# Second matmul of experts 1 to 7 by seven products of block sums, with output sums shared among DVE, ACT and POOL

## Chip, cores, metric

One core of one Trainium2 chip. The metric is the device time of one execution in microseconds (us); lower is better. Engines are named as in the profile: PE (matmul), PEld (weight load), DVE (vector), ACT (scalar), POOL (GpSimd), SP. SBUF and PSUM are the two memories in which the kernel declares its tiles; its matmuls of the expert stage write to PSUM tiles of 128 by 512 float32 ("banks").

## The reference, cut to what matters

A sparse attention (about the first 150 us, not touched in substance) makes `x` of 3072 tokens by 512. Then comes a dense mixture of 8 experts, with a routing matrix `P` that is normalised in eight rounds:

```python
def _moe_ref(x, w_gate, w1, w2):
    N, D, E, F = 3072, 512, 8, 1024
    ...                                  # P: [N, E]
    for e in range(E):
        h = np.maximum(x @ w1[e], 0.0)   # [N, F]
        ye = h @ w2[e]                   # [N, D]
        out += P[:, e:e + 1] * ye
    return out
```

## The kernel before

Every operation is a unit with a cost for each engine that may run it. A list scheduler (`Plan.order`) then fixes the order of instructions on each engine, and semaphores are added for the data.

For experts 1 to 7, `x @ w1` is already formed from seven products (the Strassen-Winograd scheme) over pairs of 512-token blocks `t1, t2` and halves of F. One "quad" is 128 columns of each half of F: seven products of two 512-column matmuls each, in place of eight. DVE sums two blocks for some products; PE adds most products in PSUM; a product that is needed twice is copied out ("snap") and added by DVE together with the relu:

```python
        def add_relu(e, p, q, blk):          # DVE: relu(PSUM + snapshot in SBUF)
            nc.vector._custom_dve(dve_ops.TENSOR_ADD_SAT, out=hidden(e, p, q, blk),
                                  in0=at[src, e, p, q][:], in1=at.pop(("snap", n, e, p, q))[:],
                                  s0=3.0e38, s1=0.0)
```

`h @ w2` is an ordinary product: for each 128 tokens, eight matmuls of 512 columns into one PSUM bank, and one DVE pass that adds `P * y` to the float32 sum `out_acc` in SBUF:

```python
        def project(e, p, c, fs, d=slice(0, DM)):
            ...
            for f in fs:
                nc.tensor.matmul(yp[:, d], lhsT=hb[e, p, q // 2][:, q % 2, blk, o:o + 128],
                                 rhs=w2s[e][:, f, d], start=(f == 0), stop=(f == KF - 1))

        def accumulate(e, p, c, d=slice(0, DM)):
            nc.vector.scalar_tensor_tensor(out=out_acc[:, t, d], in0=at.pop(("y", e, p, c, d.start))[:, d],
                                           scalar=P_sb[:, t, e:e + 1], in1=out_acc[:, t, d],
                                           op0=ALU.mult, op1=ALU.add)
```

There are 7 experts with 3 pairs of token blocks each: 21 (expert, pair). The very last 128 tokens are done in two halves of 256 columns.

The softmax here doesn't subtract the row's maximum and nothing guards it: scores larger than these inputs give would overflow.

## Time and profile before

700.39 us (median of 3; 699.55 to 701.0).

| | before |
|---|---|
| span of the profiled run | 699.8 us |
| first product of expert 1 starts | 151.9 us |
| PE work in the expert stage, about 544 us by the pitch below | 1176 matmuls of 512 columns for x @ w1, 1344 for h @ w2 (8 of them made as 16 of 256) |
| start to start, 512 columns, own weight load each | 215.8 ns |
| time PE lost beyond that pitch in the expert stage | 0.2 us |

The last two rows come from the start times of single matmuls in the trace: the interval from each start to the next, less the pitch of a matmul of that width as these starts show it (215.9 ns for 512 columns, where the 2512 intervals of the kernel before have a mean of 215.8 and a median of 216, and 109.3 for 256, where they take 109 or 110). This matters because the profile's "busy" of PE is made of modelled ends that overlap: a 512-column matmul is recorded as 379 ns long though the next starts 216 ns later, so short gaps are covered. I call this sum of lost intervals "PE gaps" below.

From the profile page of the kernel before: busy time of each engine with its share of the span, and the engines' shares of the chain of waits.

```profile
span 699.8 us, 10429 instructions
...
PE 690.7 (99%) x4128; PEld 338.4 (48%) x4130; DVE 435.5 (62%) x851; ACT 290.3 (41%) x505; POOL 91.4 (13%) x132
...
PE 91%; DMA 4%; POOL 2%; DVE 1%; issue 0%; SPq 0%; DVEq 0%; POOLq 0%
```

PE is 91% of the chain. The windows view of the same kernel (busy us of each engine with the number of instructions, granted clock, DMA) for a steady stretch of 78 us, which is one expert, and for the whole expert stage:

```profile
core 0: us, PE busy (x) PEld busy (x) DVE busy (x) ACT busy (x) POOL busy (x), PEclk, DMA share, GB/s
344.00:422.00 78.00, 78.00 (x363) 35.41 (x362) 43.31 (x65) 27.99 (x49) 1.64 (x2) 1.00 0.17 28
150.00:700.00 550.00, 546.00 (x2538) 248.07 (x2536) 311.45 (x474) 193.48 (x334) 9.81 (x12) 1.00 0.17 35
```

PE is busy all the time, DVE 43.3 of 78 us. The groups of instructions in the expert stage that the argument uses (count, busy us, mean ns of one, then idle time before):

```profile
L752 PE MATMUL yps<-w,h 128*128 128x512 f16 x1336 | 349.7, 379 | 0.0
...
L757 DVE SCALAR_TENSOR_TENSOR out_acc<-yps,P_sb,out_acc 128x512 f32<-128x512 f32 x167 | 124.7, 747 | 140.2 <-PE yps L752 140.1
L738 DVE CUSTOM_DVE_ANT_0 h<-pA,snap 128x512 f16<-128x512 f32 x84 | 57.8, 688 | 4.3 <-PE pA L721 0.3
...
L703 DVE TENSOR_TENSOR wsum<-w 128x1024 f16<-128x1024 f16 x12 | 8.2, 681 | 0.0
...
L752 PE MATMUL yps<-w,h 128*128 128x256 f16 x16 | 1.9, 273 | 0.0
```

The DVE operation (`wsum`, 1024 f16 elements) takes 0.68 us. And one line of the timeline of PE at the end of the run, with start and length:

```profile
694.20 0.93 PE L752 MATMUL yps<-w,h 128*128 128x256 f16 x7
```

Seven half-width matmuls with seven weight loads, one recorded as 273 ns, take 0.93 us: (0.93 - 0.273)/6 = 0.109 us from start to start. Half the columns, half the time.

The waits of PE in the expert stage come to this one line (who waited for what: us in total, times, longest):

```profile
...
PEld L721 <- issue: 0.2, 1, 0.2
```

### The profile page before, as it was taken

The page shows a single profiled execution, that of the slowest core. Times are in us where ns is not written, and L with a number is a line of the kernel's source. Part 1 is how long each engine was busy: PE and PEld are TensorE (multiplying, and loading weights), DVE is VectorE, ACT ScalarE, POOL GpSimd, SP SyncE. Part 2 cuts the span into 40 slices and gives each one's busy share as a digit, 9 for nine tenths or more (in the row PEclk, how much of TensorE's full clock was granted, in tenths as well). Part 3 has the DMA queues.
Part 4 walks back from the last instruction along what each step waited for, and adds up shares of the span by engine and source line. Part 5 has one row for each costly group of instructions (what it writes and reads, how often), then busy time and mean ns, then how long its engine had stood idle before and what let it go on. Part 6 is the DMA issues. An engine that isn't in the chain of part 4 may idle for free.

```text
span 699.8 us, 10429 instructions
## 1 busy us (share of the span) xinstructions
PE 690.7 (99%) x4128; PEld 338.4 (48%) x4130; DVE 435.5 (62%) x851; ACT 290.3 (41%) x505; POOL 91.4 (13%) x132
## 2 busy tenths in 40 slices
PE   8999999999999999999999999999999999999997
PEld 4666656554444444444444444444444444444443
DVE  7779877989765555475455654564555655455453
ACT  6667775554333333333333333333333333333330
POOL 7899622000000000000000000000000000000000
PEclk9999999999999999999999999999999999999999
DMA  9999933525003040204003030304003120001223
GB/s 170 160 144 145 134 64 59 93 28 93 1 1 60 1 60 1 47 14 61 1 0 61 3 58 1 60 1 61 0 1 61 19 42 1 0 1 45 91 80 146
DMA packets 95392, 36.24 MB, mean 52 GB/s; under 512 B 76016, under 2 KB 88816, under 8 KB 95344
## 3 DMA queue, kind: packets, MB, share of 16 engines
q0 software_dynamic: 77520, 25.99, 34.6%
q1 hardware_dynamic: 17152, 9.45, 5.6%
q8 instruction: 32, 0.52, 0.3%
q10 hardware_dynamic: 672, 0.15, 0.1%
q14 instruction: 16, 0.13, 0.1%
HBM read 52.45 MB, written 6.29 MB: 84 GB/s over the span
## 4 chain that ended last, share of the span: by engine, by line
PE 91%; DMA 4%; POOL 2%; DVE 1%; issue 0%; SPq 0%; DVEq 0%; POOLq 0%
PE yps L752 41%; PE pA L721 21%; PE pQ L721 10%; PE pR L721 5%; PE yps L228 5%; PE hps L223 4%; DMA w<-in_moe_w_dram 1%; DMA kT<-kst 1%; DMA Ve<-vx 1%; DMA vx<-in_v_dram 1%; PE sg L345 1%; PE av L437 1%; PE av L431 1%; PE ss L450 0%; POOL vx L287 0%; PE tkq L301 0%
## 5 line engine op out<-in xcount | busy, mean ns | idle before, releaser
L752 PE MATMUL yps<-w,h 128*128 128x512 f16 (+1 forms) x1352 | 351.5, 378 | 0.0
L757 DVE SCALAR_TENSOR_TENSOR out_acc<-yps,P_sb,out_acc 128x512 f32<-128x512 f32 (+1 forms) x169 | 125.6, 744 | 141.0 <-PE yps L752 140.9
L752 PEld LDWEIGHTS <-h 128*128 128x128 f16 x1352 | 132.3, 98 | 158.0
L219 ACT COPY snap<-pA 128x512 f32<-128x512 f32 x166 | 97.1, 585 | 143.2 <-PE pA L721 143.1
L214 ACT ACTIVATE h<-pA 128x512 f16<-128x512 f32 x83 | 49.6, 597 | 171.0 <-PE pA L721 171.0
L738 DVE CUSTOM_DVE_ANT_0 h<-pQ,snap 128x512 f16<-128x512 f32 x84 | 57.8, 688 | 77.8 <-PE pQ L721 77.2
L721 PEld LDWEIGHTS <-wsum 128*128 128x128 f16 x672 | 65.8, 98 | 79.3
L721 PE MATMUL pA<-xsum,wsum 128*128 128x512 f16 x336 | 99.6, 379 | 0.0
L721 PEld LDWEIGHTS <-w 128*128 128x128 f16 x504 | 49.3, 98 | 59.5 <-issue 0.2
L738 DVE CUSTOM_DVE_ANT_0 h<-pR,snap 128x512 f16<-128x512 f32 x84 | 57.5, 685 | 11.2 <-ACT snap L219 11.2
L738 DVE CUSTOM_DVE_ANT_0 h<-pA,snap 128x512 f16<-128x512 f32 x84 | 57.8, 688 | 4.3 <-PE pA L721 0.3
L219 ACT COPY snap<-pQ 128x512 f32<-128x512 f32 x83 | 48.5, 584 | 21.0 <-PE pQ L721 20.7
L721 PE MATMUL pQ<-xsum,wsum 128*128 128x512 f16 x168 | 50.0, 379 | 0.0
L721 PE MATMUL pA<-xsum,w 128*128 128x512 f16 x168 | 50.0, 379 | 0.0
L721 PE MATMUL pA<-xT,w 128*128 128x512 f16 x168 | 50.0, 379 | 0.0
L721 PE MATMUL pQ<-xT,wsum 128*128 128x512 f16 x168 | 50.0, 379 | 0.0
L721 PE MATMUL pR<-xT,w 128*128 128x512 f16 x168 | 50.0, 379 | 0.0
L223 PE MATMUL hps<-xT,w 128*128 128x384 f16 x256 | 48.0, 326 | 1.1 <-DMA w<-in_moe_w_dram 1.0
L228 PE MATMUL yps<-w,h 128*128 128x512 f16 x192 | 46.3, 379 | 0.0
L204 POOL DMA_DIRECT2D w<-in_moe_w_dram x11 | 8.4, 770 | 244.9 <-PE pA L721 241.9
L210 POOL DMA_DIRECT2D w<-in_moe_w_dram x8 | 7.1, 890 | 185.2 <-PE yps L752 121.3
L214 ACT ACTIVATE h<-hps 128x384 f16<-128x384 f32 x55 | 27.0, 491 | 10.2 <-PE hps L223 9.4
(127 smaller groups left out, 503.5 us busy)
## 6 DMA issues: line engine op xcount, KB each, us to landing
w<-in_moe_w_dram POOLq DMA_DIRECT2D x15, 1024.0 KB, 8.7
out_dram<-out_acc SPq DMA_DIRECT2D x23, 256.0 KB, 2.0
qst<-in_q_dram POOLq DMA_DIRECT2D x32, 96.0 KB, 5.4
vx<-in_v_dram POOLq DMA_DIRECT2D x15, 192.0 KB, 6.2
kst<-in_k_dram POOLq DMA_DIRECT2D x24, 96.0 KB, 5.7
w<-in_moe_w_dram POOLq DMA_DIRECT2D x4, 256.0 KB, 8.7
kst<-in_k_dram POOLq DMA_DIRECT2D x3, 192.0 KB, 4.6
Ve<-vx SPq DMA_DIRECT2D x32, 10.2 KB, 5.5
```

Of the source, the lines that this page charges most:

```text
L204: nc.gpsimd.dma_start(out=w1s[e][:, :, part * fw:(part + 1) * fw], in_=moe_w1[e].rearrange("(dk p) f -> p dk f", p=128)[:, :, part * fw:(p ...
L210: nc.gpsimd.dma_start(out=w2s[e][:], in_=moe_w2[e].rearrange("(fk p) d -> p fk d", p=128))
L214: nc.scalar.activation(out=out, in_=in_, func=AF.Relu, bias=0.0, scale=1.0)
L219: (nc.scalar.copy if eng == "ACT" else nc.vector.tensor_copy)(out=out, in_=in_)
L223: nc.tensor.matmul(hp[:, 0:n], lhsT=w1s[e][:, dk, f * 128:(f + 1) * 128], rhs=xT[:, dk, t0:t0 + n], start=(dk == 0), stop=(dk == KD - 1))
L228: nc.tensor.matmul(yp[:, d], lhsT=h[:, f, c * 128:(c + 1) * 128], rhs=w2s[e][:, f, d], start=(f == 0), stop=(f == KF - 1))
L345: nc.tensor.matmul(dst, lhsT=kT[r][p0:p0 + 64, g * 128:(g + 1) * 128], rhs=qT[r][p0:p0 + 64, g * 128 + l0:g * 128 + l1], start=True, stop= ...
L431: nc.tensor.matmul(av[:, o + j * VD:o + (j + 1) * VD], lhsT=em[:, j, c, :], rhs=sv[:, j, c, :], start=(cc == 0 and j == 0), stop=False, sk ...
L721: nc.tensor.matmul(dst[:], lhsT=lhsT, rhs=rhs, start=first and k == 0, stop=k == HK - 1, skip_group_check=True)
L738: nc.vector._custom_dve(dve_ops.TENSOR_ADD_SAT, out=hidden(e, p, q, blk), in0=at[src, e, p, q][:], in1=at.pop(("snap", n, e, p, q))[:], s0 ...
L752: nc.tensor.matmul(yp[:, d], lhsT=hb[e, p, q // 2][:, q % 2, blk, o:o + 128], rhs=w2s[e][:, f, d], start=(f == 0), stop=(f == KF - 1))
L757: nc.vector.scalar_tensor_tensor(out=out_acc[:, t, d], in0=at.pop(("y", e, p, c, d.start))[:, d], scalar=P_sb[:, t, e:e + 1], in1=out_acc[ ...
```

## The change

Intent: PE is the only bound, so form `h @ w2` from seven products too. The blocks are the two 512-token blocks of a pair (index 1, 2), the halves of F and the column halves of the output. For each 128 tokens `c` of both blocks there are 7 products of four 256-column matmuls: 28 x 256 = 7168 columns in place of 16 x 512 = 8192. The price is sums and more output passes: four block sums of h on DVE (`h_sum`), four sums of w2, and four passes over the float32 sum for two output tiles where there were two. One of these four, and a second for every other `c`, is shared out: ACT scales the product by P from PSUM into SBUF (`scaled`), and POOL adds it (`add_scaled`). That makes 6 POOL adds per (expert, pair), 125 in all (the last is left to DVE).

```diff
+        def h_sum(e, p, j, i):
+            h = ring(e, p, 2 * j)
+            out_, a, b, op = ((4, 1, 3, ALU.add), (5, 4, 0, ALU.subtract), (6, 2, 5, ALU.subtract),
+                              (1, 0, 1, ALU.subtract))[i]
+            nc.vector.tensor_tensor(out=h[:, :, out_, :], in0=h[:, :, a, :], in1=h[:, :, b, :], op=op)
 ... # project(): product n of four 256-column matmuls into half a bank
+        def accumulate(e, p, c, r):
+            ...
+            if r == 3:
+                o = o.rearrange("p (i d) -> p i d", i=2)
+                y = at["ya", e, p, c][:, None, 0:HD].to_broadcast([128, 2, HD])
+            else:
+                y = at["z", e, p, c][:]
+            nc.vector.scalar_tensor_tensor(out=o, in0=y, scalar=scalar, in1=o, op0=ALU.mult, op1=ALU.add)
+
+        def scaled(e, p, c, part):
+            ...
+            nc.scalar.activation(out=at[key][:, d], in_=src, func=AF.Copy, bias=0.0, scale=P_sb[:, t, e:e + 1])
+
+        def add_scaled(e, p, c, key):
+            o = out_acc[:, tok(p, c, 0), :]
+            nc.gpsimd.tensor_tensor(out=o, in0=o, in1=at.pop(("y", e, p, c, key))[:], op=ALU.add)
 ... # pair(): the units of one c
+            p1 = mul(1, [U["w2", e]], True)
+            a1 = ev("ACT", 0.46, lambda: scaled(e, p, c, 0), [p1], ya)
+            p5 = mul(5, [T(0)], True)
+            p4 = mul(4, [T(2), p5])
+            z1 = ev("DVE", 0.76, lambda: accumulate(e, p, c, 1), [p4] + first[t2], z)
+            p6 = mul(6, [T(1), a1])
+            a2 = ev("ACT", 0.46, lambda: scaled(e, p, c, 1), [p6], ya)
+            g1 = add("POOL", 1.25, lambda: add_scaled(e, p, c, False), [a2] + first[t1])
+            p3 = mul(3, [z1])
+            p7 = mul(7, [T(3), a2])
+            u3 = ev("DVE", 0.76, lambda: accumulate(e, p, c, 3), [p7, z1], ya)
+            p2 = mul(2, [p3])
+            if c % 2 and (e, p, c) != (E - 1, NPAIR - 1, 3):
+                a3 = ev("ACT", 0.68, lambda: scaled(e, p, c, 2), [p2], z)
+                z2 = add("POOL", 1.25, lambda: add_scaled(e, p, c, True), [a3, g1])
+            else:
+                z2 = ev("DVE", 0.76, lambda: accumulate(e, p, c, 0), [p2, g1], z)
 ... # cut: buffers moved to make room; in a quad, block 11 no longer needs DVE: ACT copies product 1
 ... # from PSUM to a second PSUM bank ("seed") where PE adds product 2, and ACT does the relu
```

## The prediction

> **What bounds the kernel now.** TensorE. The page gives PE 99% of the 699.8 us span at full granted clock; the chain of waits is 91% PE. In the expert stage (experts 1 to 7, from about 150 us) the windows view shows PE busy for the whole of every stretch until about 696 us. By the start times of single matmuls in the trace, 512-column expert matmuls follow each other every 215.8 ns (99th percentile 216), each with its own hidden weight load (98 ns); beyond that pitch PE loses about 0.01 us per 20 us. Nothing else costs time there: from 344 to 655 us DVE is 54% busy, ACT 36%, POOL about 2%.
>
> **What the change does to PE.** Per expert and pair of token blocks, h times w2 goes from 64 matmuls of 512 columns to 4 x 7 x 4 = 112 of 256. The x-times-w1 part stays at 56 of 512. Does a half-width matmul with its own weight load cost half? The trace has 16 such (the last token block is done in halves): they start every 109 ns, the weight load still hidden. [...] Over 21 (expert, pair): before 1176 x 0.216 + 1344 x 0.216 = 544 us; after 1176 x 0.216 + 2352 x 0.109 = 510 us. PE work falls by 34 us, all on the critical path: a bound of about 666 us.
>
> **What it adds elsewhere**, per (expert, pair), against 24.3 us of PE:
> - DVE: 8 add-relus (0.69) instead of 12; 8 block sums of h, 1024 f16 elements (0.69, as the weight sums measure); 10 accumulates (0.75) instead of 8; w2 sums join w1 sums (1.8). About 20.5 us of durations; but back-to-back DVE operations start about 0.6 us apart for a 0.69 us duration, so nearer 18.
> - ACT: 8 relus from PSUM (0.60), scaled copies (about 0.4 for 256 columns, 0.6 for 512), about 9 us; plus most of 12 seed/snapshot copies (0.585), 7 us. 16 in all.
> - POOL: 6 float32 adds of 128x512, of which the trace has none. [...]
>
> DVE about 80 to 85%, ACT 65 to 70%[...]: still PE bound, but with far less slack, longer chains (product 1, seed, 6, snapshot, 7, add-relu, 4)[...].
>
> **Where I expect losses.** (a) Expert 1, about 150 to 225 us: DVE is already 90% busy at 150 to 180 us; h and w2 sums are added: 1 to 4 us of PE gaps. (b) Steady state: 0 to 0.5 us per expert[...]. (c) The tail: last pairs have no products to interleave with, 1 us. Sum about 4 us.
>
> **Prediction: 669.5 us**, range 664 to 683. Faster by over 2% (below 686.4): 0.92; within 2%: 0.07; slower: 0.01.
>
> **What would show each step.** 256-column matmuls starting 109 ns apart; PE about 98 to 99% busy; later experts 73 us each instead of 77.8; DVE at 75 to 85%, ACT 60 to 70%; [...]gaps mainly before 230 us and at the end; 0 to 145 us unchanged within 1 us.
>
> **What would make it wrong.** [...]h sums stretched by blocking against POOL; DVE's fixed order making PE gaps in each quad; half-width matmuls paying at each bank switch or semaphore wait.

What no trace or run of this case shows is cut out of the text above, where marked: the duration forecast for a POOL add with the POOL load that followed from it, a clause of (b) on POOL adds and h sums, and remarks on the pitch of matmuls and on queues. The bound of about 666 us (699.8 - 34) and "about 4 us" of losses (a), (b) and (c) come to about 670; POOL's time was never a term of it. The durations given for scaled copies on ACT (0.4 and 0.6 us) are estimates; the trace of the kernel before has ACT copies of 512 columns from PSUM at 0.585 us and relus of 384 at 0.49. The risk "h sums stretched by blocking against POOL" had been seen in no run then; the changed kernel shows it, 71 sums longer by 65.2 us in all (below).

## More of the kernel before

The planner knows engines and PSUM banks and nothing else that could be shared:

```python
            for u in left:
                t0 = ready(u)                       # PSUM banks free?
                ...
                for e, cost in u.eng.items():
                    t = max([t0, free.get(e, 0.0)]
                            + [d.end + d.lag + (self.HOP if d.on != e else 0.0) for d in u.deps])
```

## The result

707.34 us (median of 4; 705.83 to 709.23), against 699.97 us (median of 4) for the kernel before on the same chip. The ratio is 1.0107, with a 95% interval of 1.0074 to 1.0141. Ratios here are the mean time of one kernel's fast runs over that of the other's of the same rounds, so not quite the ratio of the medians quoted. The result is correct. The prediction was 669.5 us with a range of 664 to 683; it was wrong by 38 us.

The profile after, in the same order as before. The page:

```profile
span 704.4 us, 13246 instructions
...
PE 667.4 (95%) x5130; PEld 434.1 (62%) x5131; DVE 611.2 (87%) x1033; ACT 413.0 (59%) x770; POOL 264.4 (38%) x257
...
PE 58%; DVE 28%; issue 7%; DMA 4%; POOL 2%; SPq 0%; DVEq 0%; POOLq 0%
```

The chain of waits has turned: PE 58%, DVE 28%. The windows:

```profile
core 0: us, PE busy (x) PEld busy (x) DVE busy (x) ACT busy (x) POOL busy (x), PEclk, DMA share, GB/s
344.00:422.00 78.00, 73.65 (x500) 48.45 (x499) 68.72 (x92) 44.00 (x84) 26.75 (x20) 1.00 0.17 28
150.00:700.00 550.00, 521.37 (x3529) 343.28 (x3527) 484.60 (x650) 315.18 (x599) 182.73 (x137) 1.00 0.18 34
```

In the same stretch PE is busy for 73.7 of 78 us, where it was busy for all of it; and that view still hides the gaps that overlapping modelled ends cover. DVE went from 43.3 to 68.7 of 78 us, or 88%. I had expected "DVE at 75 to 85%". The groups of instructions:

```profile
L821 POOL TENSOR_TENSOR out_acc<-out_acc,y 128x512 f32<-128x512 f32 x125 | 173.1, 1385 | 366.3 <-ACT y L817 346.3 <-issue 18.0 <-DVE h L764 1.9
...
L776 DVE TENSOR_TENSOR h<-h 128x1024 f16<-128x1024 f16 x168 | 162.2, 998 | 1.4
...
L793 PE MATMUL yps<-w,h 128*128 128x256 f16 x669 | 93.4, 273 | 1.6 <-DVE out_acc L808 1.4
...
L808 DVE SCALAR_TENSOR_TENSOR out_acc<-yps,P_sb,out_acc 128x512 f32<-128x512 f32 x126 | 93.4, 742 | 21.7 <-PE yps L793 20.6 <-PE pQ L742 0.9
...
L764 DVE CUSTOM_DVE_ANT_0 h<-pA,snap 128x512 f16<-128x512 f32 x84 | 57.2, 680 | 6.1 <-PE pA L742 5.7 <-ACT y L817 0.3
```

The 256-column matmuls are there, 2352 in all. Their cost is as forecast, as one line of PE's timeline shows (eight, of which one is recorded as 273 ns: (1.04 - 0.273)/7 = 0.110 us):

```profile
360.60 1.04 PE L793 MATMUL yps<-w2sum,h 128*128 128x256 f16 x8
```

The accumulates and add-relus keep their 0.74 and 0.68 us. The one group that is off is `h<-h` on DVE: mean 998 ns where the trace before gave 0.68 us for sums of that form. And it isn't slower throughout. A run of four such sums in the timeline of DVE, followed by the POOL line of the same time:

```profile
358.87 0.68 DVE L776 TENSOR_TENSOR h<-h 128x1024 f16<-128x1024 f16 x1
359.65 1.68 DVE L776 TENSOR_TENSOR h<-h 128x1024 f16<-128x1024 f16 x1
361.26 1.28 DVE L776 TENSOR_TENSOR h<-h 128x1024 f16<-128x1024 f16 x2
```

```profile
359.52 1.27 POOL L821 TENSOR_TENSOR out_acc<-out_acc,y 128x512 f32<-128x512 f32 x1 [1.23 <-ACT y L817]
```

The first sum takes 0.68 us. While it runs, a POOL add starts at 359.52 us. The next sum starts at 359.65 us and takes 1.68 us. The line after it is two sums together, 1.28 us: back to normal. Over the whole trace, 71 of the 233 such sums that I counted (of h, of w1 and w2, and of x as far as not in place) took more than 0.75 us, and together 65.2 us more than 0.682 us each would have. A POOL add was under way in every one of the 71. (The expectations below count 68: those over 1 us.) The ends are more telling still: each of the 71 ends 0.55 us after the add that was under way when it began, however long it had waited. It goes the other way too: 33 of the 125 adds took over 1.3 us (up to 1.83), and each of these ends about 1.13 us after a sum that began before it or at about the same moment. No add-relu or accumulate, which have one SBUF tensor input, took over 0.753 us.

What PE waited for in the expert stage:

```profile
PEld L742 <- issue: 29.4, 44, 1.2
...
PEld L793 <- DVE h L776: 13.9, 18, 1.1
...
PE pQ L742 <- DVE h L764: 11.1, 26, 0.6
...
PE yps L793 <- DVE h L776: 8.2, 12, 0.8
...
PE pA L742 <- DVE h L764: 5.3, 6, 0.9
```

("PEld ... issue" is time for which the profile shows no releaser.) The DVE names in it are the h sums and the add-relus queued behind them. By start times, PE gaps in the expert stage grew from 0.2 to 39.7 us, nearly all in 64 gaps of over 0.1 us (39.0 us).

So the account of the two profiled runs is: from the start of the first expert product to the start of the last matmul, 543.8 us before and 549.7 us after. Without the gaps that is 543.7 and 510.0 us, 34 us less, as forecast; the gaps add 39.5 us. The stage starts 1.3 us earlier, and the end after the last matmul is 0.2 us longer (4.0 and 4.2 us). The sum, 5.8 - 1.3 + 0.2 = 4.7 us, is but for rounding the difference of the spans (704.4 and 699.8). Of the 39.7 us of gaps, 3.2 us lie before 225 us and 2.3 us after the last product of expert 7; the 78 us shown above, about one expert, have 5.9 us. The saving was there in full and was lost to gaps. The question is what makes the gaps.

### The profile page after: what moved, and what is told of

Same layout as the page of the kernel before. It is cut to its first block, busy times and chain, and to the rows that moved or that the text cites. A ratio compares the mean times of both kernels' runs of the same rounds, so it can differ in the third digit from the quotient of the medians.

```text
span 704.4 us, 13246 instructions
## 1 busy us (share of the span) xinstructions
PE 667.4 (95%) x5130; PEld 434.1 (62%) x5131; DVE 611.2 (87%) x1033; ACT 413.0 (59%) x770; POOL 264.4 (38%) x257
## 4 chain that ended last, share of the span: by engine, by line
PE 58%; DVE 28%; issue 7%; DMA 4%; POOL 2%; SPq 0%; DVEq 0%; POOLq 0%
DVE h L776 13%; PE yps L793 13%; PE pA L742 13%; PE pY L793 10%; PE pQ L742 7%; DVE h L764 5%; PE hps L208 4%; PE yps L213 4%; DVE out_acc L808 4%; PE pR L742 3%; DVE w2sum L717 3%; DMA kT<-kst 1%; DMA w<-in_moe_w_dram 1%; DMA vx<-in_v_dram 1%; DMA Ve<-vx 1%
## 5 line engine op out<-in xcount | busy, mean ns | idle before, releaser
L821 POOL TENSOR_TENSOR out_acc<-out_acc,y 128x512 f32<-128x512 f32 x125 | 173.1, 1385 | 366.3 <-ACT y L817 346.3
L793 PEld LDWEIGHTS <-h 128*128 128x128 f16 x2352 | 228.4, 98 | 105.3 <-DVE h L776 13.9
L817 ACT ACTIVATE y<-pY,P_sb 128x256 f32<-128x256 f32 x168 | 79.9, 476 | 144.6 <-PE pY L793 142.8
L776 DVE TENSOR_TENSOR h<-h 128x1024 f16<-128x1024 f16 x168 | 162.2, 998 | 1.4
L808 DVE SCALAR_TENSOR_TENSOR out_acc<-yps,P_sb,out_acc 128x512 f32<-128x512 f32 x127 | 94.1, 742 | 22.0 <-PE yps L793 21.0
L793 PE MATMUL yps<-w2sum,h 128*128 128x256 f16 x672 | 100.3, 273 | 8.2 <-DVE h L776 8.2
L793 PE MATMUL pY<-w,h 128*128 128x256 f16 x672 | 100.3, 272 | 0.1
L793 PE MATMUL yps<-w,h 128*128 128x256 f16 x672 | 93.8, 273 | 1.6 <-DVE out_acc L808 1.4
L808 DVE SCALAR_TENSOR_TENSOR out_acc<-pY,P_sb,out_acc 128x512 f32<-128x512 f32 x84 | 62.5, 744 | 20.3 <-PE pY L793 17.4
L793 PE MATMUL pY<-w2sum,h 128*128 128x256 f16 x336 | 51.4, 273 | 0.7
```

The costliest lines, as they stand in the source:

```text
L776: nc.vector.tensor_tensor(out=h[:, :, out_, :], in0=h[:, :, a, :], in1=h[:, :, b, :], op=op)
L793: nc.tensor.matmul(dst[:, d], lhsT=lhsT, rhs=rhs, start=f == 0 and n in (1, 5, 2), stop=f == HF - 1, skip_group_check=True)
L808: nc.vector.scalar_tensor_tensor(out=o, in0=y, scalar=scalar, in1=o, op0=ALU.mult, op1=ALU.add)
L817: nc.scalar.activation(out=at[key][:, d], in_=src, func=AF.Copy, bias=0.0, scale=P_sb[:, t, e:e + 1])
L821: nc.gpsimd.tensor_tensor(out=o, in0=o, in1=at.pop(("y", e, p, c, key))[:], op=ALU.add)
```

## The experiments

Theory A: a POOL add that reads SBUF and a DVE operation with two SBUF inputs exclude each other, so DVE loses some 65 us standing still, and PE behind it. It is read off the trace of the changed kernel: a POOL add was under way in every one of the 71 stretched sums, and each ended 0.55 us after that add. Rival B: with or without that, DVE has too much work in a fixed order. Rival C: POOL's results come late and hold up whoever waits for them.

"Gaps" are PE gaps in the expert stage, "stretched" the sums over 0.75 us and "extra" their time over 0.682 us each.

| run | us (median) | against before | gaps | stretched | extra us | DVE busy us |
|---|---|---|---|---|---|---|
| before | 700.39 | 1 | 0.2 | 0 | 0 | 435.5 |
| changed | 707.34 | 1.0107 | 39.7 | 71 | 65.2 | 611.2 |
| e1 POOL only writes | 669.0 | 0.9553 | 2.2 | 0 | 0 | 548.1 |
| e2 adds on DVE | 690.33 | 0.9855 | 22.5 | 0 | 0 | 616.8 |
| e3 seeded, no POOL adds | 673.86 | 0.9627 | 7.1 | 0 | 0 | 575.2 |
| e4 plan knows of it | 688.8 | 0.9834 | 21.9 | 40 | 26.3 | 593.5 |
| e5 before + idle POOL adds | 699.95 | 1.0001 | 0.8 | 5 | 0.9 | 441.6 |
| e6 seeded + idle POOL adds | 694.57 | 0.9930 | 28.8 | 77 | 47.9 | 619.6 |
| e7 seeded, other order | 673.45 | 0.9627 | 7.0 | 0 | 0 | 577.3 |
| e8 POOL adds in halves | 695.19 | 0.9950 | 28.5 | 106 | 56.3 | 601.4 |

e1 to e4 shared one chip and its runs of the kernel before (median 700.96), e5 to e8 another set (699.80).

### e1: POOL writes but does not read

```diff
-            nc.gpsimd.tensor_tensor(out=o, in0=o, in1=at.pop(("y", e, p, c, key))[:], op=ALU.add)
+            y = at.pop(("y", e, p, c, key))
+            nc.gpsimd.memset(y[:], 0.0)
+            nc.gpsimd.memset(o, 0.0)
+            nc.gpsimd.memset(y[:, 0:128], 0.0)
```

Expected:

> Wrong result on purpose: each of the 126 POOL adds (reads two tensors, 1268 ns when undisturbed) is replaced by three POOL memsets of about the same total length that only write, in the same place with the same waits; the order on every engine stays that of the changed kernel. Theory A (the DVE sums with two SBUF inputs stand still while a POOL add reads SBUF: 680 ns alone, about 1680 ns when an add is under way, 68 of them in the trace of the changed kernel): no h sum over 0.75 us, DVE busy falls from 611 us by about 65 us, and the time falls to 668 to 678 us. Rival B (DVE has too much work in a fixed order and the chains are too long, blocking or not): h sums shorten but the time stays above 695 us. Rival C (POOL adds are late and hold up the output banks): as the memsets are as long, the time stays above 695 us.

Measured: 669.0 us. The result is wrong (relative error 0.73). The sums and the memsets in the groups of instructions, and the windows:

```profile
L776 DVE TENSOR_TENSOR h<-h 128x1024 f16<-128x1024 f16 x168 | 109.0, 684 | 1.4
...
L822 POOL MEMSET y<- 128x512 f32 x125 | 66.0, 528 | 360.1 <-ACT y L817 342.1 <-issue 18.0
L823 POOL MEMSET out_acc<- 128x512 f32 x125 | 65.4, 523 | 0.0
...
L824 POOL MEMSET y<- 128x128 f32 x125 | 24.7, 198 | 0.0
```

```profile
core 0: us, PE busy (x) PEld busy (x) DVE busy (x) ACT busy (x) POOL busy (x), PEclk, DMA share, GB/s
344.00:422.00 78.00, 78.00 (x541) 52.70 (x539) 63.60 (x98) 47.38 (x92) 24.19 (x62) 1.00 0.18 28
```

All h sums are back at 0.68 us, though POOL is occupied as long as before (0.528 + 0.523 + 0.198 = 1.25 us for an undisturbed 1.27) at the same places with the same waits. (There are 125 of them; the expectation says 126.) PE is busy the whole stretch, DVE 63.6 of 78 us; the gaps fall from 39.7 to 2.2 us. DVE has the same operations in the same order. So rival B falls as an explanation of most of the loss. C falls too: in the waits of this run ACT still waits 26.6 us for POOL in all, as in the changed kernel, and the gaps are gone all the same. The 29.4 us that PEld had waited with no releaser shown are 1.7 us here. What was taken away is POOL's reading. The time is also within 1 us of the forecast. The rest of that sum was right to about 2 us; that it comes so close is in part luck, as the gaps are 2.2 us where 4 were forecast, and the stage starts 1.0 us earlier than in the kernel before.

### e2: DVE does the adds itself

```diff
-            a1 = ev("ACT", 0.46, lambda: scaled(e, p, c, 0), [p1], ya)
+            a1 = ev("DVE", 0.45, lambda: acc_half(e, p, c, 0), [p1] + first[t1], ya)
-            a2 = ev("ACT", 0.46, lambda: scaled(e, p, c, 1), [p6], ya)
-            g1 = add("POOL", 1.25, lambda: add_scaled(e, p, c, False), [a2] + first[t1])
+            g1 = a2 = ev("DVE", 0.45, lambda: acc_half(e, p, c, 1), [p6], ya)
 ... # acc_half: out_acc half += P * 256 columns from PSUM; the last pass always on DVE
```

Expected:

> Correct result: no POOL adds and no scaled copies on ACT; DVE adds both halves of product 1 and of products 1+6 itself from PSUM (two operations of 256 columns) and all fourth passes. DVE nominal work goes up by about 5.3 us per expert and pair. Theory A: no h sum over 0.75 us; DVE's work, started 0.6 to 0.67 us apart, is about 22.4 of 24.3 us per pair, so the time is 675 to 695 us, faster than the changed kernel though DVE has more nominal work. Rival B (too much DVE work): slower than the changed kernel, 710 to 735 us.

Measured: 690.33 us, correct. The windows:

```profile
core 0: us, PE busy (x) PEld busy (x) DVE busy (x) ACT busy (x) POOL busy (x), PEclk, DMA share, GB/s
344.00:422.00 78.00, 76.38 (x521) 50.67 (x520) 71.87 (x122) 33.39 (x61) 1.64 (x2) 1.00 0.18 28
```

DVE is busier than in the changed kernel (71.9 against 68.7 of 78 us), and the kernel is faster by 17 us. That is hard to square with B: the busy time of DVE in the changed kernel was in part standing still. But B may have a share in this version: with no stretched sum, 22.5 us of gaps remain while DVE is busy for 92% of the stretch. No run tests that.

### e3: a version without POOL adds

PE and ACT take the sum over. Product 1 goes to the output bank; ACT copies it from PSUM to the other bank, where product 6 and 7 are added by PE; then ACT copies that sum to the bank's other half and PE adds product 4 to the first half. Each output tile then needs one DVE pass of 512 and one of 256 columns.

```diff
-            a1 = ev("ACT", 0.46, lambda: scaled(e, p, c, 0), [p1], ya)
 ... # all of scaled, add_scaled, z1, g1, a3 go
+            p5 = mul(5, [T(0), p1])
+            s1 = add("ACT", 0.46, lambda: seed_y("ACT", e, p, c, 0), [p5], pr - 105.0, opens=[ya])
 ... # cut: z is also kept for s1
+            e1 = ev("DVE", 0.45, lambda: acc_half(e, p, c, 1), [p5] + first[t2], z)
+            p6 = mul(6, [T(1), s1])
+            e2 = ev("DVE", 0.45, lambda: acc_half(e, p, c, 0), [p6] + first[t1], ya)
+            p3 = mul(3, [e1])
+            p2 = mul(2, [s1, e1])
+            z2 = ev("DVE", 0.76, lambda: accumulate(e, p, c, 0), [p2, p3, e2], z)
+            p7 = mul(7, [T(3), e2])
+            s3 = add("ACT", 0.46, lambda: seed_y("ACT", e, p, c, 1), [p7], pr, uses=[ya])
+            p4 = mul(4, [T(2), s3])
+            u3 = ev("DVE", 0.76, lambda: accumulate(e, p, c, 3), [p4, e1], ya)
 ... # cut: project() with the new banks and flags, seed_y, acc_half, one more wait for the load of w2
```

PE adds to what ACT wrote into PSUM by matmuls without the first flag (`start`): of the products of `h @ w2`, only product 1 has it, and that one goes to the output bank. That such matmuls add to ACT's copies is shown by the correct result.

Expected:

> Correct result, a version meant to beat both: no POOL adds. Product 1 goes to the output bank and ACT copies it from PSUM to the other bank, where product 6 adds to it; after product 7 ACT copies that sum into the bank's other half, and product 4 adds to the first half; so each token block needs one pass of 512 and one of 256 columns, all by DVE from PSUM. DVE about 20 of 24.3 us per pair by start-to-start times, ACT about 16. Theory A: all h sums near 0.68 us, PE gaps small, time 668 to 680 us. Rival B: PE gaps like those of the changed kernel, time 695 us or more.

Measured: 673.86 us, correct, 0.9627 of before (interval 0.9591 to 0.9662). The chain of waits, DVE's groups and the windows:

```profile
PE 88%; DMA 4%; DVE 3%; POOL 2%; ACT 1%; issue 1%; SPq 0%; POOLq 0%; DVEq 0%; ACTq 0%
```

```profile
L776 DVE TENSOR_TENSOR h<-h 128x1024 f16<-128x1024 f16 x168 | 111.7, 683 | 0.8
L814 DVE SCALAR_TENSOR_TENSOR out_acc<-yps,P_sb,out_acc 128x512 f32<-128x512 f32 x84 | 62.9, 749 | 25.3 <-PE yps L791 22.0
...
L804 DVE SCALAR_TENSOR_TENSOR out_acc<-pY,P_sb,out_acc 128x256 f32<-128x256 f32 x84 | 40.0, 476 | 3.2 <-PE pY L791 3.2
```

```profile
core 0: us, PE busy (x) PEld busy (x) DVE busy (x) ACT busy (x) POOL busy (x), PEclk, DMA share, GB/s
344.00:422.00 78.00, 77.88 (x536) 52.11 (x535) 68.50 (x115) 41.33 (x85) 1.64 (x2) 1.00 0.17 28
```

This beats both kernels. With a DVE busy for 88% of the stretch, the same share as in the changed kernel (68.5 and 68.7 of 78 us), PE is busy for 77.9 us instead of 73.7. So a DVE share of 88% is not in itself what stops PE. It is 4.9 us behind e1, and its gaps are 4.9 us longer.

### e4: the planner knows of the exclusion

Only the order: POOL adds and two-input sums may not overlap in planned time. No waits are added.

```diff
-                    t = max([t0, free.get(e, 0.0)]
+                    t = max([t0, free.get(e, 0.0), free.get("PORT", 0.0) if u.port else 0.0]
 ...
+            if u.port:
+                free["PORT"] = end + 0.05
 ... # u.port = True for the sums of x, w1, w2, h and for the POOL adds
```

Expected:

> Correct result: the changed kernel with nothing but its order changed: the planner that fixes each engine's order may no longer let a POOL add and a DVE sum with two SBUF inputs run at the same planned time. No new waits are added, so the chip may still overlap them. Theory A: fewer stretched sums than 68, and the time falls, to 680 to 698 us. Rival B: no gain, since DVE's work is the same: 700 to 715 us.

Measured: 688.8 us, correct: 18.5 us faster than the changed kernel by its order alone. 40 sums are still stretched, since the chip is free to run ahead of the plan, but by 26.3 us in place of 65.2. Less standing still, fewer gaps (21.9 us).

### e5: POOL adds in the kernel before

The other half of the test: POOL reads SBUF just as often, but DVE has almost no two-input operations.

```diff
+        def idle_add(e, p, q):
+            t = post["sb"].tile([128, BLK], FP32, tag="idle", name="idle", bufs=1)
+            h = hidden(e, p, q, 2)
+            nc.gpsimd.tensor_tensor(out=t[:], in0=h, in1=h, op=ALU.add)
 ... # one after each even quad, two after each odd one: 126
```

Expected:

> Correct result: the kernel before, with 126 idle POOL adds of 512 columns added to its expert stage (one after every even quad, two after every odd one, reading an f16 block of h, writing a scratch tile that nobody reads). Theory A (a POOL add that reads SBUF only holds up DVE operations with two SBUF inputs): the kernel before has 28 such sums of w1 in the expert stage and no h sums, and DVE has slack, so the time stays within 0.7% of the kernel before (696 to 705 us), and its add-relus and accumulates keep 0.69 and 0.75 us. Rival (POOL work slows the core whatever DVE does): over 1% slower.

Measured: 699.95 us, correct, a ratio of 1.0001 (0.9986 to 1.0016). Groups and windows:

```profile
L746 POOL TENSOR_TENSOR idle<-h 128x512 f32<-128x512 f16 x126 | 131.0, 1040 | 385.0 <-ACT h L214 355.8 <-DVE h L738 24.4 <-DVE h L216 1.4
L738 DVE CUSTOM_DVE_ANT_0 h<-pQ,snap 128x512 f16<-128x512 f32 x84 | 57.8, 688 | 72.3 <-PE pQ L721 72.1
```

```profile
core 0: us, PE busy (x) PEld busy (x) DVE busy (x) ACT busy (x) POOL busy (x), PEclk, DMA share, GB/s
344.00:422.00 78.00, 78.00 (x363) 35.31 (x362) 43.75 (x65) 27.62 (x48) 20.63 (x21) 1.00 0.17 28
```

POOL goes from 1.6 to 20.6 us of the stretch, the add-relus keep 0.69 us, PE is busy all the time. POOL work costs nothing here. (DVE also has slack here, 43.8 of 78 us busy, so this run alone does not tell whether the adds are harmless for want of sums to catch or because DVE can afford it.) Five w1 sums were caught (0.85 us each). One other group moved: the first scaling of the sums, a DVE operation with one SBUF input and no PSUM one, took 479 ns on average in the kernel before, and here:

```profile
L771 DVE TENSOR_SCALAR out_acc<-out_acc,P_sb 128x512 f32<-128x512 f32 x20 | 12.2, 644 | 0.0
```

Five of them took 0.94 to 1.30 us, each with a POOL add under way. Why these are caught too, with one SBUF tensor input, is not shown.

### e6: idle POOL adds in the seeded version

```diff
+            for _ in range(1 + q % 2):
+                add("POOL", 1.27, lambda: idle_add(e, p, q), [c21])
```

Expected:

> Correct result: the same 126 idle POOL adds put into the seeded version (673.9 us), whose results nobody waits for. They start when the last block of a quad is ready, which is when the h sums start too. Theory A: 60 to 90 sums stretched by about 1 us each, DVE busy up by 60 to 90 us, time 695 to 725 us, though nothing on the path waits for POOL. Rival C (late POOL results, not blocking): within 1% of 673.9 us.

Measured: 694.57 us, correct: 20.7 us slower than e3 though nobody waits for what POOL computes, apart from the reuse of h two pairs later; no wait for POOL appears in its expert stage. Groups, and the chain of waits:

```profile
L782 DVE TENSOR_TENSOR h<-h 128x1024 f16<-128x1024 f16 x168 | 152.4, 924 | 0.8
L775 POOL TENSOR_TENSOR idle<-h 128x512 f32<-128x512 f16 x126 | 149.4, 1186 | 367.3 <-ACT h L199 354.0 <-ACT pY L204 5.2 <-issue 4.6
```

```profile
PE 76%; DVE 18%; issue 3%; DMA 1%; ACT 1%; SPq 0%; DVEq 0%; ACTq 0%
```

77 sums stretched, as many as expected, and DVE is back in the chain with 18% (3% in e3). I expected 695 us or more and DVE 60 to 90 us busier; it was 44 us, as these POOL adds read f16 and last 1.04 us (the mean in e5), and a stretched sum lost 47.9/77 = 0.62 us, not 1. With e5 this is both sides: the adds cost 21 us where there are many two-input sums (and little slack on DVE) and nothing where there are almost none (and much slack). Rival C falls again.

### e7: the seeded version in another order

The planner's durations replaced by measured start-to-start times, the rest as a delay of the result.

```diff
 ... # cut: the planner adds the delay where a PSUM bank is used again
+        took = {("DVE", 0.69): 0.6, ("DVE", 0.7): 0.61, ("DVE", 0.76): 0.67, ("DVE", 0.45): 0.4, ("DVE", 0.5): 0.41,
+                ("ACT", 0.6): 0.49, ("ACT", 0.46): 0.3, ("ACT", 0.75): 0.6}
 ... # for each DVE and ACT unit of the expert stage:
+                u.eng = {k: took[k, c] for k, c in u.eng.items()}
+                u.lag = 0.09
```

Expected:

> Correct result: the seeded version with another order only: the planner reckons the engine time of DVE and ACT operations by the start-to-start times that the traces show (DVE 0.60 for a sum, 0.67 for an accumulate, 0.40 for half of one; ACT 0.49 and 0.30) plus 0.09 us until the result is there. The seeded run still lost 7.1 us in PE gaps in the expert stage. Theory: some of these gaps come from an order made with too long durations; 667 to 673 us. Rival: the gaps come from too few banks or the chains; 672 to 676 us.

Measured: 673.45 us, correct, the same ratio as e3 (0.9627), gaps 7.0 us. No gain, so the durations in the plan were not what kept the last 7 us. Whether they come from the number of banks or from the length of the chains was not separated and stays open.

### e8: POOL adds in halves

```diff
-            nc.gpsimd.tensor_tensor(out=o, in0=o, in1=at.pop(("y", e, p, c, key))[:], op=ALU.add)
+            y = at.pop(("y", e, p, c, key))
+            for d in (slice(0, HD), slice(HD, DM)):
+                nc.gpsimd.tensor_tensor(out=o[:, d], in0=o[:, d], in1=y[:, d], op=ALU.add)
```

Expected:

> Correct result: the changed kernel with each POOL add made as two adds of 256 columns. Theory A: [...]a stretched sum takes about 1.2 us instead of 1.7; if a sum is stretched by one half only, DVE busy falls by some 30 us and the time to 680 to 697 us; if the halves follow each other before the sum gets in, nothing is gained (700 to 710 us). I expect the first, at 0.6. Rival C (late POOL results): two adds take longer in all, so slower than 707 us.

Measured: 695.19 us, correct. Groups:

```profile
L823 POOL TENSOR_TENSOR out_acc<-out_acc,y 128x256 f32<-128x256 f32 x250 | 228.9, 931 | 298.8 <-ACT y L817 282.4 <-issue 15.3 <-DVE h L776 0.6
L776 DVE TENSOR_TENSOR h<-h 128x1024 f16<-128x1024 f16 x168 | 159.9, 985 | 1.4
```

(The 1.2 us of the expectation is an estimate: 0.68 us and half of the 1 us by which the caught sum shown above, of 1.68 us, is longer.) The time fell into the expected range, but not by the expected way. DVE busy fell by 10 us, not 30: more sums were caught (106), each for less (56.3/106 = 0.53 us on average; most took 1.1 to 1.2 us). PE gaps fell more than the standing still did, by 11 us. That shorter stops are covered more easily by the full banks would explain it, but that is an argument and not shown. POOL's adds took longer in all (228.9 us busy, against 173.1 in the changed kernel), and still the kernel got faster; that speaks against C once more.

## Why the prediction was wrong, point by point

- *PE bound before, gap-free:* right. PE gaps of 0.2 us in 544 us.
- *"PE work falls by 34 us", half-width matmuls every 109 ns:* right. Median 109 ns from start to start in the changed kernel, 2352 of them, no cost at bank switches (a median of 109 ns over the 515 intervals in which the next matmul writes to a tile of another name).
- *Durations of the added operations:* right for ACT's copies in size (0.48 and 0.69 us, said 0.4 and 0.6), and for the accumulates (0.74). POOL adds took 1.27 us undisturbed. Right for the h sums undisturbed (0.68). Wrong for the h sums as they ran: mean 0.998.
- *"DVE about 80 to 85%":* 88% was measured, of which the stretch is part: 65.2 us of the 484.6 that DVE was busy from 150 to 700 us.
- *Where it failed: term (b), "Steady state: 0 to 0.5 us per expert".* "h sums stretched by blocking against POOL" was listed under "What would make it wrong" and given no size; no more than "about 4 us" was booked for losses in all. The steady state measured 5.9 us of PE gaps per expert in place of 0 to 0.5, and all gaps 39.7 us in place of about 4. The risk named was the right one and this term was mis-sized: 71 stretched sums (59 of h, 12 of weights), about 0.9 us each, 65 us of DVE. Taking away POOL's reading alone (e1) gave 669.0 us where 669.5 had been forecast.
- *What its size comes to.* The trace before had no POOL add, so neither the blocking nor its length could be read from it; one run with such adds beside such sums, as in e6, would have shown both. An estimate with the times measured since, per (expert, pair): 6 adds of 1.27 us and 8 h sums in 24.3 us. POOL adds are then under way for 7.6/24.3 = 31% of the time, so by chance alone 31% of the 168 h sums are caught, 53 of them; at up to a whole add each, up to 67 us of DVE. (59 h sums were caught and lost 53 us.) The trace had 54% DVE load before and I had forecast 80 to 85% after. Of the 510 us that I gave the stage, 67 us are 13%: DVE at up to 93 to 98%, and the forecast of a PE bound would have looked unsafe.
- *"0 to 145 us unchanged":* nearly; the first expert product starts 149.3 us after the first matmul in the changed kernel and 150.6 us after it before.
- *(a) Expert 1, 1 to 4 us:* in range, 3.2 us of gaps up to 225 us, but in part by the blocking: e1 has 1.0 us there.
- *(c) Tail 1 us:* too little; after the last product of expert 7 there are 2.3 us of gaps (0.7 in e1), and the end after the last matmul grew by 0.2 us.

Of the rivals, B (too much work in a fixed order) explains little of the changed kernel (2.2 us of gaps remain in e1) but what remains in e2, with DVE at 92% and no stretched sum, may be of its kind; that is not shown. C is refuted by e1, e6 and e8.

## What to carry to other kernels

When work that reads SBUF is moved to POOL to relieve DVE, ask which DVE operations read two SBUF tensors (or are like the first scalings in e5) at the same time: here the "free" engine stopped the very one it was to relieve (71 sums, 65.2 us of DVE). Give such blocking a size before believing a bound: share of time that one is under way, times the number of the other, times the hold. And tell a stretched operation from a costly one: a bimodal duration in a group (0.68 and 1.68 us here) with a mean in between is a sign of waiting inside the instruction, which the idle column doesn't show (1.4 us in all before the h sums of the changed kernel, against 168 x (998 - 682) ns = 53 us of stretch).
